# All sums of the block products on VectorE, stepped between its reads of PSUM, and one product moved behind two others

## The chip, the cores and the metric

The kernel runs on one core of one Trainium2 chip. The metric is the device time in microseconds of one execution. Before the change it is 494.15 us (median of 3 runs, 493.62 to 495.61). Profiles are of one execution; their times count from the first instruction, and the profiled span is 491.8 us.

TensorE (PE) multiplies matrices and writes to PSUM. VectorE (DVE) and ScalarE (ACT) read PSUM and work elementwise. GpSimd (POOL) works elementwise on SBUF only, and here it also issues the indirect transfers that fetch and store rows by number. SyncE (SP) issues the weight loads. Each engine runs its own instructions in the order of the program and waits for others at semaphores.

## What is computed

An attention layer of the RWKV-5 kind gives 3072 tokens of 384 features. A router then picks one of 8 experts for each token by cosine similarity, and the expert is a network of two layers:

```python
N, D, E, F = (3072, 384, 8, 1024)
...
for e in range(E):
    mask = expert_idx == e
    h = np.maximum(x[mask] @ w1[e], 0.0)
    out[mask] = gate_w[mask, None] * (h @ w2[e])
```

All values are 32-bit floats. The change concerns only these last two products, which take the kernel from about 205 us on to its end.

## The kernel before

The experts are handled one after the other as eight blocks, `blocks[0]` to `blocks[7]`, each with room for so many gathered tokens: 256 in the first two, then 448, 416, 416, 384, 384 and 384. Both layers are computed as 2x2 block products with **seven products instead of eight**, in the manner of Strassen and Winograd: sums and differences of the quarters of each operand are formed first, and the products of these are added up in PSUM and by VectorE. Only the first block's hidden layer is done plainly (`plain`), and the tokens above 256 in the second layer (`rest`).

The sums are these. S belongs to the left operand, T to the right one:

```python
def combined(eng, other, t1, t2, t3, t4, b11, b12, b21, b22):
    eng.tensor_sub(t1, b12, b11)
    other.tensor_sub(t3, b22, b12)
    eng.tensor_sub(t2, b22, t1)
    eng.tensor_sub(t4, b21, t2)

def summed_up(eng, other, s1, s2, s3, s4, a11, a12, a21, a22):
    other.tensor_add(s1, a21, a22)
    eng.tensor_sub(s2, s1, a11)
    other.tensor_sub(s3, a11, a21)
    eng.tensor_sub(s4, a12, s2)
```

Four places call them. In the profile their tiles are called Tx, Sw, Tw and Sh:

```python
def turn(self):       # transposes tokens, then Tx: sums of the tokens, for the hidden layer
    ...
        combined(nc.vector, nc.vector, *self.T, b[0][0], b[0][1], b[1][0], b[1][1])

def weigh(self):      # Sw: sums of w1, 128x512 each
    ...
    summed_up(nc.gpsimd, nc.vector, *self.S, a[0][0], a[1][0], a[0][1], a[1][1])

def weigh_out(self):  # Tw: sums of w2, 128x768 each
    ...
    combined(nc.gpsimd, nc.gpsimd, *self.T, b[0][0], b[0][1], b[1][0], b[1][1])

def halves(self):     # Sh: sums of the hidden layer's result hT, 128x512 each
    ...
    self.S = [k.cb.tile([128, NF // 2, 128], F32, name=f"Sh{j}", tag=f"Sh{j}") for j in range(4)]
    summed_up(nc.vector, nc.vector, *self.S, a[0][0], a[0][1], a[1][0], a[1][1])
```

The hidden layer goes through the weights in two rounds; `add` is a product accumulated into a bank of PSUM:

```python
def hidden(self):
    ...
    for f in range(0, NF // 2, 2):
        g = f + NF // 2
        p1, p6, p5, p7 = bank(), bank(), bank(), bank()
        add(p1, w1[:, 0, :], f, x[:, 0, one], first=True)
        p1s = kept("p1")
        nc.scalar.copy(p1s, p1)
        add(p6, self.S[1], f, self.T[1], first=True)
        u2 = kept("u2")
        vec.tensor_add(u2, p6, p1s)                      # L1049
        add(p5, self.S[0], f, self.T[0], first=True)
        p15 = kept("p15")
        vec.tensor_add(p15, p5, p1s)                     # L1052
        add(p7, self.S[2], f, self.T[2], first=True)
        p157 = kept("p157")
        vec.tensor_add(p157, p7, p15)
        add(p1, w1[:, 1, :], f, x[:, 1, one])
        add(p1, w1[:, 2, :], f, x[:, 2, one])
        nc.scalar.activation(self.hT[:, f : f + 2, one], p1, ACT.Relu)
        add(p5, self.S[3], f, x[:, 1, two])              # needs L1052's read of p5
        add(p5, w1[:, 2, :], f, x[:, 2, two])
        vec.tensor_add(self.hT[:, f : f + 2, two], p5, u2)
        relu(f, two)
        add(p7, w1[:, 1, :], g, self.T[3])
        ...
```

The second layer for the first 256 tokens:

```python
def out(self, between):
    ...
    y = [k.gp.tile([128, DM], F32, name="y", tag="y", bufs=4) for _ in range(2)]
    p1, p6, p5, p7 = bank(), bank(), bank(), bank()
    add(p1, h[:, lo, 0:128], w2[:, lo, half], first=True)
    ...
    nc.scalar.copy(p1s, p1)
    add(p6, S[1], T[1], first=True)
    vec.tensor_add(u2, p6, p1s)
    nc.scalar.mul(u21, u2, gate[1])
    nc.scalar.mul(u20, u2, gate[0])
    add(p5, S[0], T[0], first=True)
    nc.scalar.mul(p5s, p5, gate[1])
    add(p7, S[2], T[2], first=True)
    vec.scalar_tensor_tensor(u3, p7, gate[1], u21, ALU.mult, ALU.add)   # L1110
    vec.tensor_add(y[1][:, other], u3, p5s)
    add(p7, h[:, hi, 128:256], T[3])                                    # needs L1110's read of p7
    vec.scalar_tensor_tensor(y[1][:, half], p7, gate[1], u21, ALU.mult, ALU.add)
    self.put(1, y[1])
    add(p1, h[:, hi, 0:128], w2[:, hi, half])
    nc.scalar.mul(y[0][:, half], p1, gate[0])
    add(p5, S[3], w2[:, hi, other])
    vec.scalar_tensor_tensor(y[0][:, other], p5, gate[0], u20, ALU.mult, ALU.add)
    self.put(0, y[0])
    between()                        # turn of the block after next
    if self.n > 256:
        self.rest(self.n - 256)
```

The order of the whole, with `at(i)` being block i where there is one:

```python
for i in range(E):
    blocks[i].halves()
    for b in at(i + 1):
        b.hidden()
    for b in at(i + 2):
        b.weigh()
    first_weights(i + 3)
    blocks[i].out(lambda: [b.turn() for b in at(i + 2)])
    for b in at(i + 3):
        b.gather()
    for b in at(i + 1):
        b.weigh_out()
    second_weights(i + 2)
```

Of the kernel before, what the change touches and what calls it, by code (L numbers as in the profile page):

```python
# [1 line left out]

# [7 lines left out]
F32 = mybir.dt.float32  # L10
# [15 lines left out]
NF = F // 128  # L26
# [788 lines left out]
class Early:  # L815
# [44 lines left out]
    def out(self, to):  # L860
        k, nc, ps = self.k, self.k.nc, self.ps
        y = k.work.tile([128, DM], F32, name="earlyy", tag="xd")
        nc.vector.tensor_scalar_mul(y, ps, self.gate)
        nc.gpsimd.indirect_dma_start(
            out=k.out[:, :], out_offset=IndirectOffsetOnAxis(ap=to[:, self.col], axis=0), in_=y[:, :], in_offset=None,
            bounds_check=N - 1, oob_is_err=False,
        )
# [90 lines left out]
class Block:  # L958
# [14 lines left out]
    def turn(self):  # L973

        k, nc, n = self.k, self.k.nc, self.n
        self.xT = k.xtp.tile([128, NK, TM * 128], F32, name="xTe", tag="xTe")
        for m in range(NK):
            ps = k.ps.tile([128, TM * 128], F32, name="ps", tag="ps")
            for t, (G, _, _, here) in enumerate(self.tiles):
                nc.tensor.transpose(  # L980
                    ps[:, t * 128 : t * 128 + here], G[0:here, m * 128 : (m + 1) * 128], k.ident[0:here, 0:here]
                )
            nc.scalar.copy(self.xT[:, m, 0:n], ps[:, 0:n])
        if self.rank != TURN[0]:
            b = [[self.xT[:, m, s * n // 2 : (s + 1) * n // 2] for s in range(2)] for m in range(2)]
            self.T = [k.xtp.tile([128, TM * 64], F32, name=f"Tx{j}", tag=f"Tx{j}")[:, 0 : n // 2] for j in range(4)]
            combined(nc.vector, nc.vector, *self.T, b[0][0], b[0][1], b[1][0], b[1][1])

    def weigh(self):

        k, nc, w1 = self.k, self.k.nc, self.w1
        a = [[w1[:, m, s * F // 2 : (s + 1) * F // 2] for s in range(2)] for m in range(2)]
        self.S = [k.cb.tile([128, F // 2], F32, name=f"Sw{j}", tag=f"Sw{j}") for j in range(4)]
        summed_up(nc.gpsimd, nc.vector, *self.S, a[0][0], a[1][0], a[0][1], a[1][1])

    def weigh_out(self):

        k, nc, w2 = self.k, self.k.nc, self.w2
        b = [[w2[:, f * NF // 2 : (f + 1) * NF // 2, s * DM // 2 : (s + 1) * DM // 2] for s in range(2)] for f in range(2)]
        self.T = [k.cb.tile([128, NF // 2, DM // 2], F32, name=f"Tw{j}", tag=f"Tw{j}") for j in range(4)]  # L1000
        combined(nc.gpsimd, nc.gpsimd, *self.T, b[0][0], b[0][1], b[1][0], b[1][1])

    def plain(self):

# [8 lines left out]
                )  # L1013
            nc.scalar.activation(self.hT[:, f, 0:n], ps[:, 0:n], ACT.Relu)

    def hidden(self):

        k, nc, n, w1, x = self.k, self.k.nc, self.n, self.w1, self.xT
        half, vec = n // 2, self.k.nc.vector
        one, two = slice(0, half), slice(half, n)  # L1020
        self.hT = k.hp.tile([128, NF, TM * 128], F32, name="hT", tag="hT")

        def bank():
            return k.ps.tile([128, TM * 128], F32, name="ps", tag="ps")[:, 0 : 2 * half].rearrange("p (j t) -> p j t", j=2)

        def kept(name):
            t = k.ev.tile([128, TM * 128], F32, name=name, tag=name)
            return t[:, 0 : 2 * half].rearrange("p (j t) -> p j t", j=2)

        def add(ps, weights, f, moving, first=False):  # L1030
            for j in range(2):
                nc.tensor.matmul(  # L1032
                    ps[:, j, :], weights[:, (f + j) * 128 : (f + j + 1) * 128], moving,
                    start=(first and j == 0), stop=True, skip_group_check=True,
                )

        def relu(f, cols):
            h = self.hT[:, f : f + 2, cols]
            nc.scalar.activation(h, h, ACT.Relu)  # L1039
# [13 lines that stand above are left out]
            add(p7, self.S[2], f, self.T[2], first=True)  # L1053
            p157 = kept("p157")
            vec.tensor_add(p157, p7, p15)
            add(p1, w1[:, 1, :], f, x[:, 1, one])
            add(p1, w1[:, 2, :], f, x[:, 2, one])
            nc.scalar.activation(self.hT[:, f : f + 2, one], p1, ACT.Relu)
            add(p5, self.S[3], f, x[:, 1, two])
# [4 lines that stand above are left out]
            add(p7, w1[:, 2, :], g, x[:, 2, one])  # L1064
            vec.tensor_add(self.hT[:, g : g + 2, one], p7, u2)
            relu(g, one)
            add(p6, w1[:, 2, :], g, x[:, 2, two])
            vec.tensor_add(self.hT[:, g : g + 2, two], p6, p157)
            relu(g, two)

    def halves(self):

        k, nc = self.k, self.k.nc
        a = [[self.hT[:, f * NF // 2 : (f + 1) * NF // 2, t * 128 : (t + 1) * 128] for f in range(2)] for t in range(2)]
        self.S = [k.cb.tile([128, NF // 2, 128], F32, name=f"Sh{j}", tag=f"Sh{j}") for j in range(4)]
        summed_up(nc.vector, nc.vector, *self.S, a[0][0], a[0][1], a[1][0], a[1][1])

    def out(self, between):

        k, nc, S, T, h, w2 = self.k, self.k.nc, self.S, self.T, self.hT, self.w2  # L1080
        vec, half = nc.vector, slice(0, DM // 2)
# [22 lines left out]
        vec.tensor_add(u2, p6, p1s)  # L1104
        nc.scalar.mul(u21, u2, gate[1])
        nc.scalar.mul(u20, u2, gate[0])
        add(p5, S[0], T[0], first=True)
        nc.scalar.mul(p5s, p5, gate[1])
        add(p7, S[2], T[2], first=True)
        vec.scalar_tensor_tensor(u3, p7, gate[1], u21, ALU.mult, ALU.add)  # L1110
        vec.tensor_add(y[1][:, other], u3, p5s)
        add(p7, h[:, hi, 128:256], T[3])
        vec.scalar_tensor_tensor(y[1][:, half], p7, gate[1], u21, ALU.mult, ALU.add)  # L1113
        self.put(1, y[1])
        add(p1, h[:, hi, 0:128], w2[:, hi, half])
        nc.scalar.mul(y[0][:, half], p1, gate[0])
        add(p5, S[3], w2[:, hi, other])
        vec.scalar_tensor_tensor(y[0][:, other], p5, gate[0], u20, ALU.mult, ALU.add)
        self.put(0, y[0])
        between()  # L1120
        if self.n > 256:
            self.rest(self.n - 256)

    def rest(self, n):

        k, nc, h, w2 = self.k, self.k.nc, self.hT, self.w2
        mm = nc.tensor.matmul
        if n % 128:

# [9 lines left out]
        for t, (_, _, gate, here) in list(enumerate(self.tiles))[2:]:  # L1139
            ps = k.ps.tile([128, TM * 128], F32, name="ps", tag="ps")  # L1140
            if n % 128:
                at = slice((t - 2) * 128, (t - 2) * 128 + here)
                for m in range(NK):
                    nc.tensor.transpose(ps[0:here, m * 128 : (m + 1) * 128], yT[:, m, at], k.ident)
            else:
                for f in range(NF):
                    mm(ps[:, 0:DM], h[:, f, t * 128 : (t + 1) * 128], w2[:, f, :], start=(f == 0), stop=(f == NF - 1))  # L1147
            y = k.gp.tile([128, DM], F32, name="y", tag="y", bufs=4)
            nc.vector.tensor_scalar_mul(y[0:here], ps[0:here, 0:DM], gate[0:here])  # L1149
            self.put(t, y)  # L1150

    def put(self, t, y):
# [4 lines left out]
        )  # L1157


def combined(eng, other, t1, t2, t3, t4, b11, b12, b21, b22):  # L1160

    eng.tensor_sub(t1, b12, b11)  # L1162
    other.tensor_sub(t3, b22, b12)  # L1163
    eng.tensor_sub(t2, b22, t1)  # L1164
    eng.tensor_sub(t4, b21, t2)


def summed_up(eng, other, s1, s2, s3, s4, a11, a12, a21, a22):

    other.tensor_add(s1, a21, a22)  # L1170
    eng.tensor_sub(s2, s1, a11)  # L1171
    other.tensor_sub(s3, a11, a21)
    eng.tensor_sub(s4, a12, s2)


def experts(k):
# [18 lines left out]
    for b in blocks[0:2]:  # L1195
        b.gather()
        b.turn()
    blocks[1].weigh()
    blocks[0].plain()
    first_weights(2)  # L1200
    blocks[2].gather()
    blocks[0].weigh_out()
    for i in range(E):
        blocks[i].halves()
        for b in at(i + 1):
            b.hidden()
        for b in at(i + 2):
            b.weigh()
        first_weights(i + 3)
        blocks[i].out(lambda: [b.turn() for b in at(i + 2)])  # L1210
        for b in at(i + 3):
            b.gather()
        for b in at(i + 1):
            b.weigh_out()
        second_weights(i + 2)


# [184 lines left out]
```

## Time and profile before

| engine | busy, us | share of the span | instructions |
|---|---|---|---|
| TensorE | 437.6 | 89% | 3266 |
| TensorE's weight loads | 393.5 | 80% | 3266 |
| VectorE | 258.3 | 53% | 574 |
| GpSimd | 254.6 | 52% | 306 |
| ScalarE | 169.2 | 34% | 488 |

The profile page cuts the span into 40 slices of 12.3 us; a digit is the busy share of an engine in a slice in tenths, and PEclk is the clock that TensorE was granted. A line of a timeline has the start in us, the duration in us, the engine, the line of the kernel, the operation, what is written and read, how many instructions were merged, and in brackets how long the engine had been idle before and what ended that wait. A matmul of the program shows as two records, since its operands are 32-bit floats. A table of waits has the waiting engine and line, the one waited for, the sum in us, how often, and the longest. Idle time of an engine that nobody waits for costs nothing.

### The profile page before, as it was taken

What the parts mean: (1) busy time and instruction counts of PE and PEld (TensorE: products, weight loads), DVE (VectorE), ACT (ScalarE), POOL (GpSimd) and SP (SyncE); (2) the same over time, 40 slices, a digit from 0 to 9 for tenths busy, and PEclk for the clock granted to TensorE, in tenths of its full rate; (3) what the DMA queues carried; (4) which work ended last, traced back from release to release, by engine and by line L of the source; (5) the groups of instructions that cost most, each with busy time, mean ns of one, the idle gap of its engine ahead of it and who ended that gap; (6) DMA issues with size and microseconds to landing.
All of it is one profiled execution on the core that took longest, in us unless ns stands there. A gap on an engine that the chain in (4) does not pass through costs nothing. (4 is left out here: it accounts for less than half of the span.)

```text
span 491.8 us, 8850 instructions
## 1 busy us (share of the span) xinstructions
PE 437.6 (89%) x3266; PEld 393.5 (80%) x3266; DVE 258.3 (53%) x574; ACT 169.2 (34%) x488; POOL 254.6 (52%) x306
## 2 busy tenths in 40 slices
PE   8789999999999989995999999999989989399490
PEld 3678989888988887785999898998889887398370
DVE  3556766656667743446464543345464563931720
ACT  2376666555655540221234233132132122022010
POOL 7766586776668312482266463176185193701710
PEclk9999999999999999995999999999999999889797
DMA  8665555456530780231362613424442410400000
GB/s 178 129 140 124 125 130 112 105 109 130 130 81 33 283 312 12 81 110 73 129 209 74 217 47 144 129 85 145 161 113 99 145 48 33 144 1 16 31 37 19
DMA packets 93799, 54.36 MB, mean 111 GB/s; under 512 B 76937, under 2 KB 88380, under 8 KB 93746
## 3 DMA queue, kind: packets, MB, share of 16 engines
q1 hardware_dynamic: 89024, 43.85, 32.3%
q0 software_dynamic: 3296, 9.44, 5.7%
q8 instruction: 28, 0.46, 0.4%
q10 hardware_dynamic: 1426, 0.41, 0.3%
q14 instruction: 25, 0.20, 0.1%
HBM read 44.45 MB, written 9.63 MB: 110 GB/s over the span
## 5 line engine op out<-in xcount | busy, mean ns | idle before, releaser
L1154 POOL DMA_INDIRECT out_dram<-y,to x25 | 27.6, 1106 | 115.0 <-DVE y L1113 46.9
L1032 PE MATMUL ps<-xTe,w 128*128 128x192 f32 (+3 forms) x336 | 65.4, 336 | 0.0
L1032 PEld LDWEIGHTS ps<-xTe,w 128*128 128x128 f32 x336 | 58.5, 200 | 0.5
L305 ACT ACTIVATE xd<-V,diag 128x48 f32<-128x48 f32 x192 | 45.8, 321 | 19.3 <-DVE diag L297 14.9
L337 DVE TENSOR_TENSOR AT<-at,umask 128x512 f32<-128x512 f32 x48 | 30.9, 685 | 34.2 <-PE at L333 34.2
L1094 PE MATMUL ps<-Tw,Sh 128*128 128x192 f32 x192 | 34.4, 338 | 9.2 <-POOL Tw L1164 9.2
L1094 PEld LDWEIGHTS ps<-Tw,Sh 128*128 128x128 f32 x192 | 32.7, 197 | 10.4 <-POOL Tw L1164 10.4
L1039 ACT ACTIVATE hT<-hT 128x384 f32<-128x384 f32 (+3 forms) x42 | 22.0, 523 | 54.5 <-DVE hT L1061 39.9
L367 POOL TENSOR_TENSOR state<-state,wpow 48x192 f32<-48x192 f32 x40 | 20.4, 509 | 28.2 <-DVE state L363 26.7
L333 PE MATMUL at<-RT,KT 48*128 48x128 f32 x384 | 27.9, 285 | 4.4 <-ACT KT L322 3.4
L333 PEld LDWEIGHTS at<-RT,KT 48*128 48x128 f32 x384 | 23.3, 187 | 9.3 <-ACT KT L322 5.0
L898 POOL DMA_INDIRECT G<-xs,take x25 | 26.0, 1040 | 8.9 <-issue 7.0
L1032 PE MATMUL ps<-Tx,Sw 128*128 128x192 f32 (+3 forms) x168 | 29.8, 327 | 0.0
L1032 PEld LDWEIGHTS ps<-Tx,Sw 128*128 128x128 f32 x168 | 27.7, 191 | 0.2
L1032 PE MATMUL ps<-xTe,Sw 128*128 128x192 f32 (+3 forms) x56 | 13.2, 362 | 16.3 <-DVE p L1052 16.3
L383 PE MATMUL y<-AT,V 128*48 128x128 f32 x384 | 25.9, 277 | 0.0
L291 POOL TENSOR_TENSOR KU<-KU,Rpad 128x384 f32<-128x384 f32 x24 | 24.0, 1001 | 1.9
L282 POOL TENSOR_TENSOR Kpad<-K,kpow 128x384 f32<-128x384 f32 x23 | 23.0, 1001 | 3.5 <-DVE kpow L100 2.3
L1032 PEld LDWEIGHTS ps<-xTe,Sw 128*128 128x128 f32 x56 | 10.0, 209 | 18.1 <-issue 18.1
L290 POOL TENSOR_TENSOR KU<-K,u_bc 128x384 f32<-128x384 f32 x24 | 24.0, 1000 | 0.3 <-DVE diag L297 0.3
L1171 POOL TENSOR_TENSOR Sw<-Sw,w 128x512 f32<-128x512 f32 x7 | 11.4, 1631 | 24.2 <-DVE Sw L1170 16.2
L1094 PE MATMUL ps<-w,hT 128*128 128x192 f32 x128 | 23.4, 326 | 0.0
(234 smaller groups left out, 978.6 us busy)
## 6 DMA issues: line engine op xcount, KB each, us to landing
w<-in_moe_w_dram SPq DMA_DIRECT2D x16, 1536.0 KB, 6.9
K<-in_k_dram SPq DMA_DIRECT2D x24, 192.0 KB, 3.3
V<-in_v_dram SPq DMA_DIRECT2D x24, 192.0 KB, 3.6
xs<-X SPq DMA_DIRECT2D x24, 192.0 KB, 2.0
Rpad<-in_r_dram SPq DMA_DIRECT2D x23, 192.0 KB, 3.6
G<-xs,take POOLq DMA_INDIRECT x27, 3.1
out_dram<-y,to POOLq DMA_INDIRECT x25, 2.6
Rpad<-in_r_dram ACTq DMA_DIRECT2D x1, 192.0 KB, 3.8
```

Source lines behind the costliest of these rows:

```text
L282: k.nc.gpsimd.tensor_mul(k.Kpad[i % len(k.Kpad)][:, :, 0:D], k.loaded[i][0], k.kpow)
L290: nc.gpsimd.tensor_mul(KU, K, k.u_bc)
L291: nc.gpsimd.tensor_mul(KU, KU, R[:, :, 0:D])
L305: k.nc.scalar.mul(xd[:, h, :], V[:, h, :], diag[:, h : h + 1])
L333: nc.tensor.matmul(at[s][:, p, :], KT[rows, p, :], RT[rows, p, :], start=True, stop=True)
L337: nc.vector.tensor_mul(a, at[s], k.umask[:, None, :].to_broadcast([128, NP, C]))
L383: mm(y[s * DP : s * DP + D, p, :], V[:, 2 * p + s, :], AT[s][:, p, :], start=(c == 0 and p == 0), stop=True, skip_group_check=True,)
L898: nc.gpsimd.indirect_dma_start(out=G[0:n, :], out_offset=None, in_=k.xs[:, :], in_offset=IndirectOffsetOnAxis(ap=take[0:n], axis=0), bound ...
L1032: nc.tensor.matmul(ps[:, j, :], weights[:, (f + j) * 128 : (f + j + 1) * 128], moving, start=(first and j == 0), stop=True, skip_group_che ...
L1039: nc.scalar.activation(h, h, ACT.Relu)
L1094: nc.tensor.matmul(ps, a[:, f, :], b[:, f, :], start=(first and f == 0), stop=(f == NF // 2 - 1), skip_group_check=True)
L1154: k.nc.gpsimd.indirect_dma_start(out=k.out[:, :], out_offset=IndirectOffsetOnAxis(ap=k.to[0:here, j : j + 1], axis=0), in_=y[0:here, :], i ...
```

## The change

All sums go to VectorE. Those of a block's first weights (Sw) and of the hidden result (Sh) are no longer formed in one run of four: the functions become generators, and `out` takes single steps from them between VectorE's reads of PSUM. The sums of the second weights (Tw) are stepped in the same way by `hidden` of the following block. GpSimd is left with the transfers alone. Sh gets two buffers, since the next block's are now formed while the present ones are read. In `out` the product that goes on in p7's bank moves to the end, behind two others. The scaling of the remaining rows in `rest` moves from VectorE to ScalarE, and the last block's remainder is done ahead of its `out`. The aim is that no run of sums stands in front of VectorE's reads of PSUM, and that TensorE need not wait for GpSimd.

The core of the diff (cuts marked with `...`):

```diff
     def weigh(self):
...
-        summed_up(nc.gpsimd, nc.vector, *self.S, a[0][0], a[1][0], a[0][1], a[1][1])
+        yield from summed_up(nc.vector, *self.S, a[0][0], a[1][0], a[0][1], a[1][1])
     def weigh_out(self):
...
-        combined(nc.gpsimd, nc.gpsimd, *self.T, b[0][0], b[0][1], b[1][0], b[1][1])
+        yield from combined(nc.vector, *self.T, b[0][0], b[0][1], b[1][0], b[1][1])
-    def hidden(self):
+    def hidden(self, steps):
...
             vec.tensor_add(p157, p7, p15)
+            do(steps, 1)
...
             vec.tensor_add(self.hT[:, g : g + 2, two], p6, p157)
             relu(g, two)
+            do(steps, 1)
     def halves(self):
...
-        self.S = [k.cb.tile([128, NF // 2, 128], F32, name=f"Sh{j}", tag=f"Sh{j}") for j in range(4)]
-        summed_up(nc.vector, nc.vector, *self.S, a[0][0], a[0][1], a[1][0], a[1][1])
-
-    def out(self, between):
+        self.S = [k.cb.tile([128, NF // 2, 128], F32, name=f"Sh{j}", tag=f"Sh{j}", bufs=2) for j in range(4)]
+        yield from summed_up(nc.vector, *self.S, a[0][0], a[0][1], a[1][0], a[1][1])
+
+    def out(self, steps):
...
         nc.scalar.mul(u20, u2, gate[0])
+        do(steps, 2)
         add(p5, S[0], T[0], first=True)
         nc.scalar.mul(p5s, p5, gate[1])
         add(p7, S[2], T[2], first=True)
         vec.scalar_tensor_tensor(u3, p7, gate[1], u21, ALU.mult, ALU.add)
         vec.tensor_add(y[1][:, other], u3, p5s)
-        add(p7, h[:, hi, 128:256], T[3])
-        vec.scalar_tensor_tensor(y[1][:, half], p7, gate[1], u21, ALU.mult, ALU.add)
-        self.put(1, y[1])
+        do(steps, 3)
         add(p1, h[:, hi, 0:128], w2[:, hi, half])
...
         self.put(0, y[0])
-        between()
-        if self.n > 256:
-            self.rest(self.n - 256)
+        do(steps, 3)
+        add(p7, h[:, hi, 128:256], T[3])
+        vec.scalar_tensor_tensor(y[1][:, half], p7, gate[1], u21, ALU.mult, ALU.add)
+        self.put(1, y[1])
...
-            nc.vector.tensor_scalar_mul(y[0:here], ps[0:here, 0:DM], gate[0:here])
+            nc.scalar.mul(y[0:here], ps[0:here, 0:DM], gate[0:here])
...
+def do(steps, count=4):
+    for _ in range(count):
+        next(steps, None)
...
     for i in range(E):
-        blocks[i].halves()
+        doubled = blocks[i].weigh_out()
         for b in at(i + 1):
-            b.hidden()
+            b.hidden(doubled)
+        do(doubled)
+        if i == E - 1:
+            blocks[i].rest()
+        ready = [b.weigh() for b in at(i + 2)] + [b.halves() for b in at(i + 1)]
+        blocks[i].out(itertools.chain(*ready))
+        first_weights(i + 3)
         for b in at(i + 2):
-            b.weigh()
-        first_weights(i + 3)
-        blocks[i].out(lambda: [b.turn() for b in at(i + 2)])
+            b.turn()
+            do(b.Tx)
+        if 256 < blocks[i].n and i < E - 1:
+            blocks[i].rest()
         for b in at(i + 3):
             b.gather()
-        for b in at(i + 1):
-            b.weigh_out()
         second_weights(i + 2)
```

`combined` and `summed_up` lose their second engine and yield after each sum. Ahead of the loop, the second block's Sw and the first block's Sh are formed in whole on VectorE, and the first block's Tw is left to the loop.

## The prediction

> **What bounds the kernel now.** I read the share of each engine first, then the chain that ended last, then TensorE's own waits, and last the timelines of TensorE, VectorE and GpSimd around the longest of those waits. The first three rows show that TensorE is the fullest engine and that VectorE and GpSimd are only half full, so no amount of work taken off those two shortens anything by itself:
>
> ```profile
> span 491.8 us, 8850 instructions
> PE   8789999999999989995999999999989989399490
> POOL 7766586776668312482266463176185193701710
> PEclk9999999999999999995999999999999999889797
> ```
>
> The holes in the PE row (slices 19, 35 and 38) are the places to look at, and the granted clock falls in or right after each. The table of TensorE's waits over the expert stage (200 to 482 us) has engine and line waited for, sum in us, times, longest:
>
> ```profile
> PE ps L1032 <- DVE p L1052: 16.3, 6, 7.4
> PE ps L1094 <- POOL Tw L1164: 9.2, 3, 6.2
> PE ps L1094 <- DVE v L1110: 5.4, 8, 0.7
> ```
>
> So 30.9 us of the stage are waits of TensorE on VectorE and GpSimd. TensorE's timeline places the long ones and shows what follows them (start, us, then the idle time in brackets):
>
> ```profile
> 227.38 1.19 PE L1032 MATMUL ps<-xTe,Sw 128*128 128x128 f32 x4 [7.29 <-DVE p L1052]
> ...
> 418.25 0.81 PE L1032 MATMUL ps<-xTe,w 128*128 128x192 f32 x4
> ...
> 429.70 1.62 PE L1032 MATMUL ps<-xTe,Sw 128*128 128x192 f32 x4 [7.38 <-DVE p L1052]
> ...
> 465.09 5.62 PE L1094 MATMUL ps<-Tw,Sh 128*128 128x192 f32 x24 [6.19 <-POOL Tw L1164]
> ```
>
> The same four matmul records take 0.81 us at 418 and 1.62 us at 429.70: a long hole is paid twice, once as idle time and once in a slow clock after it. Why VectorE is late at 429 is in the timelines of VectorE and GpSimd:
>
> ```profile
> 418.99 0.68 DVE L1170 TENSOR_TENSOR Sh<-hT 128x512 f32<-128x512 f32 x1
> 419.71 0.69 DVE L1171 TENSOR_TENSOR Sh<-Sh,hT 128x512 f32<-128x512 f32 x1
> 420.31 6.10 DVE L1172 TENSOR_TENSOR Sh<-hT 128x512 f32<-128x512 f32 x1
> 426.34 2.28 DVE L1173 TENSOR_TENSOR Sh<-hT,Sh 128x512 f32<-128x512 f32 x1
> ...
> 420.53 1.82 POOL L1162 TENSOR_TENSOR Tw<-w 128x768 f32<-128x768 f32 x1
> 422.30 1.81 POOL L1163 TENSOR_TENSOR Tw<-w 128x768 f32<-128x768 f32 x1
> 424.06 1.80 POOL L1164 TENSOR_TENSOR Tw<-w,Tw 128x768 f32<-128x768 f32 x1
> 425.94 2.14 POOL L1165 TENSOR_TENSOR Tw<-w,Tw 128x768 f32<-128x768 f32 x1
> ```
>
> A sum of 0.68 us takes 6.10 us while GpSimd forms its sums. Behind it stand VectorE's reads of PSUM (L1049, L1052), and TensorE waits for L1052. VectorE's sums are short when GpSimd has none; its reads of PSUM keep their 0.54 to 0.62 us either way. The two engines' sums exclude each other.
>
> **What the Trainium skill says.** "SBUF — State Buffer", section "Who interferes with whom", says that a VectorE instruction with two SBUF inputs contends with a GpSimd instruction that reads SBUF, and that the loser blocks fully instead of sharing. The trace agrees (6.10 us against 0.68), but for who goes first: the record of the blocked sum begins at 420.31, before GpSimd's at 420.53. "TensorE: Matmul & The Clock Gate", section "Part 1: The HAM clock gate", says that an idle window of about 3.4 us halves the clock: the waits of 6.2 to 7.4 us are followed by doubled times, the ones of 1.6 us and less are not. "SBUF — State Buffer", section "SBUF: two separate sides", warns that VectorE can hold up GpSimd's writing of DMA descriptors. In the trace one gather among VectorE's sums took 1.50 us on GpSimd instead of 1.00; VectorE's sums beside it kept 0.68.
>
> **The change part by part.** A product of four matmuls shows as 8 records, 1.30 us at 192 columns (374.00 to 375.30). TensorE's matmuls are the same in number and shape; only their order in the second layer changes. So everything gained must come out of its holes.
>
> 1. *First block's wait (227.38).* Removed: 7.29 us idle. From 227.38 to 237.07, 64 records took 9.69 us; at the later rate (12 in 1.34 us, 0.112 each) they take 7.2, so the slow clock cost 2.5. What stays: the half-sums of the first block can only start after the last Relu (ends 217.83). Four at a spacing of 0.61 us (279.72 to 280.33) end at 220.3, and two reads of PSUM at 0.35 end at 221.0. TensorE is ready at 219.9: 1.1 us of wait stay, too short for the slow clock. Gain 7.3 + 2.5 - 1.1 = **8.7**.
> 2. *Last block's hidden layer (429.70).* Idle 7.38. The first 12 records took 3.98 us instead of 1.95, the next 12 took 2.09: 2.2 of slow clock. The half-sums now lie inside the output product of the block before. Gain **9.6**.
> 3. *Last output product (465.09).* Idle 6.2; from 465.09 to 471.38 6.29 us, against 4.73 for the same work at 443.57: 1.6. The last block's weight sums now go on VectorE, four at an estimated 0.87 us (128x192 sums are spaced 0.28, 128x512 ones 0.61, so about 1.0 ns per column), 3.5 us in all, while TensorE does two plain remainders of 5.2 us each. Gain **7.8**.
> 4. *Two smaller waits for GpSimd's Tw* (367.78 and 403.29): 1.44 + 1.60. The Tw sums are now stepped through the hidden layer before. Gain **3.0**.
> 5. *Waits on L1110*, eight of 0.67 us: the product that goes on in p7's bank started before VectorE had read p7. Two other products (2.6 us) now lie between; the read takes 0.42. Gain **5.4**.
> 6. *Small waits on L1052* (0.20, 0.29, 0.54, 0.55), made by the half-sums right ahead of u2. Gain **1.6**.
> 7. *Tail.* The last evacuation is half a row (0.42 us) instead of a whole one (0.62). Gain **0.2**.
>
> Sum: 8.7 + 9.6 + 7.8 + 3.0 + 5.4 + 1.6 + 0.2 = 36.3.
>
> What is added: 46 sums on VectorE (2 of Sw in each of 7 blocks, 4 of Tw in each of 8), and 9 row scalings of 0.6 us leave it for ScalarE. For a block of 384 tokens VectorE then has 12 reads of PSUM at 0.56 us (6.7), 8 sums at 0.61 and 4 at 0.87 (8.4), the token sums (1.4) and the output's reads (2.0): 18.5 us in a block of 35.3 (349.80 to 385.14). It does not become the bound. Nor do the steps stand in the way one by one. In a hidden step TensorE needs 2.6 us for the four first products and 1.3 for p1's rest before it needs L1052's read of p5. The step of 0.87 us from the round before ends 1.5 us in, u2 then ends at 2.0 and L1052 at 2.5, against 3.9. In the output product, with u2 read 3.2 us in, two steps end at 4.5 and p7 is complete at 5.3; then u3 and y end at 6.2, three steps at 8.1, the read of p5 at 8.5, three more steps at 10.4 and y[1] at 10.8. TensorE has gone on to transposes at 9.3, whose first Tx comes about 0.4 us late; that matters only in the two blocks without a remainder, by 0.1 at most. I allow **0.7** for all such small waits and semaphores. 36.3 - 0.7 = 35.6, and 494.15 - 35.6 = **458.5 us**.
>
> **The rivals.**
> - *VectorE's order becomes the wait.* With 12 sums of 0.6 to 0.9 us between its reads of PSUM in a block (it had 6), one bad place costs up to 0.9 us; twice a block over 7 blocks that is 12 us, so about 470. For it: these waits are in the profile even now (0.2 to 0.55 on L1052). Against it: the slacks above, 1.4 us in the hidden layer.
> - *GpSimd's transfers are held up by VectorE's sums.* Against: gathers and weight loads come about a block ahead of use (the weights land 6.8 us after issue), and the writes have no reader. Only the last write is on the end, with no sum beside it. Worth 0 to 1 us.
> - *The excess goes another way*: TensorE without holes is throttled, or the slow clock stays after the first wait. From 237 to 300 it was busy 60.91 of 63 us at a clock of 1.00, so I expect no throttle; the slow clock would cost 2.5, giving 461.
> - *The transfers bound it.* The DMA share is 0.27 to 0.45 in the stretches between 217 and 418 us; compressing them by a seventh leaves room.
>
> **Range and chances.** The parts 2, 3 and 5 (22.8 us) follow from order alone and I hold them nearly certain; part 1 and the allowance carry the doubt, some 2 us towards faster and 5 towards slower. So 455 to 463. To come out less than 2% faster (above 484.3) nearly three quarters of the gain would have to be lost: 0.02; slower 0.01.
>
> **What would show it.** TensorE's waits in the stage: L1052 down from 16.3 us to about 1, once, in the first block; the ones on Tw and on the read in the output product gone. The sums on VectorE: all Sh and Sw at 0.68, Tw near 0.95, no 6.10. Busy time: TensorE down by the 6.3 us of slow clock, GpSimd down by some 80 us (32 Tw sums x 1.9 and 14 Sw sums x 1.43). The PE row without holes after slice 20. Wrong would be: a new wait of TensorE on a step or on Tx in each block; Tw at well over 1 us; VectorE's sums stretched by GpSimd's transfers, too.

## The result and the profile after

The changed kernel takes **456.88 us** (median of 4 runs, 456.70 to 460.14) against 494.0 before (median of 4 runs, 493.62 to 495.61): a ratio of **0.9258**, 95% interval 0.9212 to 0.9305. The forecast was 458.5 us, with a range of 455 to 463. The time is right, but in part by luck: two errors in the steps that make it up, each of about 4 us, cancel.

In six of the thirteen profiles of this document, the changed kernel's among them but not that of before, TensorE's clock dips once between 175 and 185 us, ahead of everything that was changed, and 2 to 3 us go there. So I compare stages, from the first plain matmul to TensorE's last one, and from there to the end.

The head of the page after the change (share of engines; then the rows of 40 slices, now of 11.5 us):

```profile
span 458.0 us, 8806 instructions
PE 429.9 (94%) x3266; PEld 391.2 (85%) x3266; DVE 257.1 (56%) x611; ACT 174.0 (38%) x497; POOL 178.4 (39%) x260
PE   8879999999999998999999999999999999999970
POOL 7765676685675732144004114113113113200310
```

The holes of the PE row after slice 19 are gone. GpSimd lost 76.2 us (254.6 to 178.4), where some 80 were forecast. VectorE has 37 instructions more and is busy 1.2 us less (258.3 to 257.1): the time of the sums it took over is about that of the stretching and the row scalings that it lost. TensorE's waits in the same stage (columns as before):

```profile
PE ps L1033 <- DVE p L1053: 1.1, 1, 1.1
PE ps L981 <- DVE earlyy L864: 0.7, 1, 0.7
PE ps L1147 <- ACT yT L1141: 0.5, 3, 0.2
```

L1053 is the former L1052. Of the 30.9 us of waits on VectorE and GpSimd, 1.1 are left, once, in the first block; the other two lines were there before. TensorE's timeline at the places of the three long holes:

```profile
224.04 0.71 PE L1033 MATMUL ps<-xTe,Sw 128*128 128x128 f32 x4 [1.12 <-DVE p L1053]
...
400.29 0.81 PE L1033 MATMUL ps<-xTe,w 128*128 128x192 f32 x4
...
404.19 0.81 PE L1033 MATMUL ps<-xTe,Sw 128*128 128x192 f32 x4
...
435.31 4.06 PE L1097 MATMUL ps<-Tw,Sh 128*128 128x192 f32 x24
```

No bracket stands behind the last two, and the 24 records take 4.06 us where they took 5.62. VectorE's part is in the lists of the tiles (least, median and greatest duration in ns, then first and last start):

```profile
L1175 DVE TENSOR_TENSOR Sh<-hT x8: 682/684/685, 222.0 to 420.8; 128x512 f32<-128x512 f32 x8
L1167 DVE TENSOR_TENSOR Tw<-w,Tw x8: 948/948/951, 229.0 to 426.0; 128x768 f32<-128x768 f32 x8
```

L1175 is the sum that took 6.10 us. Now all eight take 0.68, and Tw takes 0.95 on VectorE against 1.8 to 2.1 on GpSimd. The short waits on L1110 are gone, too. The product that goes on in p7's bank, in the last block but one, before and after:

```profile
448.30 1.54 PE L1094 MATMUL ps<-Tw,hT 128*128 128x192 f32 x8 [0.67 <-DVE v L1110]
...
422.39 1.46 PE L1097 MATMUL ps<-Tw,hT 128*128 128x192 f32 x8
```

From the first plain matmul to TensorE's last product the stage took 273.8 us before and 233.6 after: **40.2 us less, 4 more than the parts 1 to 6 of the forecast** (36.1). From TensorE's last product to the end it took 11.1 us before and **14.7** after: 3.6 more, where the forecast had 0.2 less. GpSimd's timeline shows that end, first before the change and then after it:

```profile
477.07 0.97 POOL L1154 DMA_INDIRECT out_dram<-y,to  x1 [2.42 <-DMA out_dram<-y,to]
481.61 0.97 POOL L1154 DMA_INDIRECT out_dram<-y,to  x1 [3.57 <-DVE y L1149]
...
435.12 0.97 POOL L1157 DMA_INDIRECT out_dram<-y,to  x1 [3.06 <-ACT y L1152]
443.20 0.97 POOL L1157 DMA_INDIRECT out_dram<-y,to  x1 [7.12 <-DVE y L1120]
447.61 0.97 POOL L1157 DMA_INDIRECT out_dram<-y,to  x1 [3.44 <-DVEq L1267]
```

TensorE ends at 443.27, VectorE has the last half row ready at 443.73, but the last write starts at 447.61. It stood behind the write of 443.20: the profile names VectorE's sequencer as what ended that wait, but the kernel's third profile, below, has "3.84 <-DMA out_dram<-y,to" at the same place. Before the change the last write started 0.93 us after TensorE's end (481.61 against 480.68).

### The profile page after: what moved, and what is told of

Its sections match the earlier page's. It is cut to its first block, busy times and chain, and to the rows that moved or that the text cites. A ratio compares the mean times of both kernels' runs of the same rounds, so it can differ in the third digit from the quotient of the medians.

```text
span 458.0 us, 8806 instructions
## 1 busy us (share of the span) xinstructions
PE 429.9 (94%) x3266; PEld 391.2 (85%) x3266; DVE 257.1 (56%) x611; ACT 174.0 (38%) x497; POOL 178.4 (39%) x260
## 5 line engine op out<-in xcount | busy, mean ns | idle before, releaser
L1157 POOL DMA_INDIRECT out_dram<-y,to x25 | 30.5, 1220 | 179.7 <-issue 91.8
L1033 PE MATMUL ps<-xTe,w 128*128 128x192 f32 (+3 forms) x336 | 62.9, 327 | 0.0
L1033 PEld LDWEIGHTS ps<-xTe,w 128*128 128x128 f32 x336 | 55.9, 190 | 0.5
L338 DVE TENSOR_TENSOR AT<-at,umask 128x512 f32<-128x512 f32 x48 | 30.9, 686 | 34.2 <-PE at L334 34.2
L1097 PE MATMUL ps<-Tw,Sh 128*128 128x192 f32 x192 | 32.5, 326 | 0.0
L1097 PEld LDWEIGHTS ps<-Tw,Sh 128*128 128x128 f32 x192 | 31.4, 190 | 0.0
L1050 DVE TENSOR_TENSOR u<-ps,p 128x384 f32<-128x384 f32 (+3 forms) x14 | 7.8, 557 | 31.7 <-PE ps L1033 30.9
L490 ACT COPY xT<-xp 128x384 f32<-128x384 f32 x24 | 11.5, 479 | 31.8 <-PE xp L488 31.8
L384 PEld LDWEIGHTS y<-AT,V 128*48 128x48 f32 x384 | 19.8, 122 | 3.0
```

The costliest lines, as they stand in the source:

```text
L338: nc.vector.tensor_mul(a, at[s], k.umask[:, None, :].to_broadcast([128, NP, C]))
L384: mm(y[s * DP : s * DP + D, p, :], V[:, 2 * p + s, :], AT[s][:, p, :], start=(c == 0 and p == 0), stop=True, skip_group_check=True,)
L1033: nc.tensor.matmul(ps[:, j, :], weights[:, (f + j) * 128 : (f + j + 1) * 128], moving, start=(first and j == 0), stop=True, skip_group_che ...
L1097: nc.tensor.matmul(ps, a[:, f, :], b[:, f, :], start=(first and f == 0), stop=(f == NF // 2 - 1), skip_group_check=True)
L1157: k.nc.gpsimd.indirect_dma_start(out=k.out[:, :], out_offset=IndirectOffsetOnAxis(ap=k.to[0:here, j : j + 1], axis=0), in_=y[0:here, :], i ...
```

## The experiments

**One half of the change at a time.** The first kernel keeps the new order and steps, and puts the sums back on the engines that formed them before (two of Sw and all of Tw on GpSimd):

```diff
-    yield eng.tensor_sub(s2, s1, a11)
+    yield (slow or eng).tensor_sub(s2, s1, a11)      # slow is GpSimd for Sw
...
-        yield from combined(nc.vector, *self.T, b[0][0], b[0][1], b[1][0], b[1][1])
+        yield from combined(nc.gpsimd, *self.T, b[0][0], b[0][1], b[1][0], b[1][1])
```

> The changed kernel's order and steps, but the sums that GpSimd had before (two of Sw, all four of Tw) are on GpSimd again. Theory A (order and engine are both needed): the long stretched half-sums ahead of the hidden layer are gone, since they lie in the output product, but Tw at 1.8 us each on GpSimd stand behind its gathers and end late, so TensorE waits on Tw ahead of some output products (3 such waits before, 9.2 us) and some VectorE sums are still stretched over 1 us: 460 to 468 us. Theory B (the order is all): 457, as the changed kernel. Theory C (the two engines' exclusion is all): back near 485 to 494.

Measured: 475.29 us, ratio to before 0.9588 (0.9551 to 0.9626). TensorE's waits:

```profile
PE ps L1033 <- DVE p L1053: 7.3, 1, 7.3
PE ps L1097 <- POOL Tw L1167: 5.7, 4, 2.1
```

The waits on Tw came as expected. What the expectation of 460 to 468 forgot is the first block: its half-sums stand ahead of the hidden layer in the new order, too, GpSimd forms that block's Tw at the same time, and one sum is stretched to 5.31 us again. The first hidden layer takes 19.63 us as before (19.82), not 11.21. So both theories of a single cause fall: order alone gives about half. Its stage is 24.9 us shorter than before, and its end is 4.5 us longer. The forecast held that the parts 2, 3 and 5 follow from order alone. The last hidden layer takes 14.30 us, as in the changed kernel, and no wait on the read of p7 is listed, but the last output product still waits 1.4 us for Tw, instead of 6.2.

The second kernel does the opposite: all sums on VectorE, in their old places.

```diff
-    summed_up(nc.gpsimd, nc.vector, *self.S, a[0][0], a[1][0], a[0][1], a[1][1])
+    summed_up(nc.vector, nc.vector, *self.S, a[0][0], a[1][0], a[0][1], a[1][1])
-    combined(nc.gpsimd, nc.gpsimd, *self.T, b[0][0], b[0][1], b[1][0], b[1][1])
+    combined(nc.vector, nc.vector, *self.T, b[0][0], b[0][1], b[1][0], b[1][1])
```

> The kernel before with all sums on VectorE, in their old places in runs of four, and nothing else changed. Theory A (the engine alone gives little, the order gives the rest): no sum is stretched over 1 us, but four Tw (3.5 us) and four Sh (2.4 us) stand in one run of 5.9 us ahead of each hidden layer from the third block on; L1052 ends near 7.6 us into the layer and TensorE needs it at 3.9 to 4.5: six waits of 3 to 4 us (about 22), one of some 3.4 ahead of the last output product, one of 1.1 in the first, and the eight of 0.67 stay. Removed are about 33 us, added 28 plus some slow clock: 484 to 494. Theory B (the exclusion of the two engines is all): 462 to 466, with no wait of TensorE over 1.2 us.

Measured: 506.3 us, ratio to before 1.0209 (1.0157 to 1.026): slower than before, beyond even theory A's 494. Its waits:

```profile
PE ps L1032 <- DVE p L1052: 24.2, 7, 4.1
PE ps L1094 <- DVE v L1110: 4.6, 8, 0.6
PE ps L1094 <- DVE Sh L1171: 4.4, 1, 4.4
```

The sums are all at 0.68 and 0.95 us, so the stretching is gone, and yet TensorE idles 33 us. The waits are those expected; what was sized too small is the slow clock. TensorE's timeline at one of them:

```profile
319.41 0.87 PE L1032 MATMUL ps<-xTe,w 128*128 128x208 f32 x4
...
327.61 1.75 PE L1032 MATMUL ps<-xTe,Sw 128*128 128x208 f32 x4 [3.81 <-DVE p L1052]
...
444.90 0.92 PE L1032 MATMUL ps<-xTe,Sw 128*128 128x192 f32 x4 [3.87 <-DVE p L1052]
445.65 0.81 PE L1032 MATMUL ps<-xTe,w 128*128 128x192 f32 x4
```

A wait of 3.8 us can already be followed by doubled times. Six of the seven waits on L1052 last 3.57 to 4.05 us (the first lasts 1.12), and after five of them the granted clock is 0.50 to 0.62 for some 5 us. After the sixth, the 3.87 us at 444.90, it stays at 1.00. The hidden layers together took 137.7 us against 101.9 in the changed kernel: 35.8 more, with 24.2 of idle time listed (23.1 more). **The engine without the order is a loss; the gain of 37 us needs both.**

**The moved product alone**, in the kernel before:

```diff
-        add(p7, h[:, hi, 128:256], T[3])
-        vec.scalar_tensor_tensor(y[1][:, half], p7, gate[1], u21, ALU.mult, ALU.add)
-        self.put(1, y[1])
         add(p1, h[:, hi, 0:128], w2[:, hi, half])
...
         self.put(0, y[0])
+        add(p7, h[:, hi, 128:256], T[3])
+        vec.scalar_tensor_tensor(y[1][:, half], p7, gate[1], u21, ALU.mult, ALU.add)
+        self.put(1, y[1])
```

> The kernel before with one thing changed: the product that goes on in p7's bank is moved to the end of the output product. Theory A (a short wait costs its idle time): 8 x 0.67 = 5.4 us less, 488.6. Theory B (a short wait costs more than the profile's idle time, because the pipeline has to fill again): the output product took 10.02 us with the wait in the first block before the change and 9.10 after it, so 0.92 each, 7.4 us less, 486.6. In both the eight waits of 0.67 are gone from the table. The last two writes of the second-layer product come closer together, but the remainder follows them, so nothing is lost at the end.

Measured: 492.34 us, ratio 0.9941 (0.9915 to 0.9967): 1.6 to 4.2 us less, and both totals missed. In the output products that nothing else disturbs theory B holds: 9.10 us instead of 10.01. But part of it is given back. TensorE comes to Tw earlier and waits longer for it (10.6 us instead of 9.2), and from TensorE's last product to the end it takes 13.5 us instead of 11.1. My sentence that nothing is lost at the end was wrong by 2.4 us, where the forecast's end is off by 3.8.

**Do the places of the steps matter?** The four Tw sums of a block in one run, or in two pairs:

```diff
             vec.tensor_add(p157, p7, p15)
-            do(steps, 1)                    # pairs: do(steps, 2)
...
             relu(g, two)
-            do(steps, 1)
+            do(steps, 4)                    # pairs: do(steps, 2)
```

> The changed kernel, but the four Tw sums of a block stand in one run at the end of the hidden layer's first round, instead of one at each of four places. Theory A (the places matter, and the slack can be worked out): four sums take 3.5 us, so in a block of 384 tokens they end 4.1 us into the second round, u2 and L1053 follow at 5.2, and TensorE needs L1053's read at 3.9: a wait of 1.3 in each of three blocks, 1.1 in the two of 416, 0.9 in that of 448, 2.0 in the first; with 0.2 for filling the pipeline again some 10 us more, 467. Theory B (VectorE is half empty, so the places are of no account): no change. The second round's waits on L1053 in TensorE's table tell them apart.

> The changed kernel, but the four Tw sums stand in two pairs, both in the first round of the hidden layer. Theory A (the slack is about 1.4 us in a block of 384): the second pair ends 2.4 us into the second round, L1053 at 3.45, needed at 3.9: no wait but in the first block, where it is 0.3; so at most 0.5 us more. If each added sum ahead of a read cost its own time (theory B), 0.9 us in each of seven blocks, 6 us more.

Measured on the same chip as the unaltered kernel's second run (459.0 us): 470.32 us for the run of four, and 460.13 for the pairs. Their stages are 12.4 and 0.9 us longer. The run of four has this line among TensorE's waits:

```profile
PE ps L1033 <- DVE p L1053: 10.0, 8, 2.1
```

Its six later hidden layers grew by 1.1 (448 tokens), 1.3 and 1.3 (416) and 1.5 three times (384); worked out were 0.9, 1.1 and 1.3, and 0.2 for refilling. The first grew by 3.8, where 2.0 and 0.2 were worked out: its second wait, of 2.1 us, was followed by a clock of 0.61. The pairs' 0.9 us lie in the first hidden layer as well, where 0.3 us of wait were worked out and 0.6 measured. So theory A holds but for the first block. The slack of 1.4 us is real, and an engine that is 56% busy can still cost 12 us by the place of four instructions.

**The end.** First the last block's remainder behind its output product again, as before the change:

```diff
-        if i == E - 1:
-            blocks[i].rest()
...
-        if 256 < blocks[i].n and i < E - 1:
+        if 256 < blocks[i].n:
```

> The changed kernel, but the last block's remainder is done after its output product again. Theory A (the writes of rows stand in a line): in the changed kernel the last two writes follow each other by 4.4 us (443.20 and 447.61), because each write waits until the one before has landed, and VectorE had the second half ready at 443.73. With the remainder last, 5.2 us of TensorE lie between, as before the change (477.07 and 481.61): the last write starts about 0.9 us after TensorE's last product instead of 4.3, so 3.4 us less, 453.5 us. Theory B (what is longer at the end is the closing of the program, the same in any order): no change, 456.9. Theory C (the remainder ahead of the last product was needed to hide the last Tw sums): VectorE forms them in 3.5 us during the remainder of the block before, 5.2 us, so no wait is expected; if it were, 1 to 2 us would come back.

Measured: 457.33 us, ratio 0.9227 (0.9196 to 0.9257), which overlaps the changed kernel's interval. GpSimd's timeline:

```profile
437.93 0.97 POOL L1157 DMA_INDIRECT out_dram<-y,to  x1 [5.99 <-DVE y L1120]
442.72 0.97 POOL L1157 DMA_INDIRECT out_dram<-y,to  x1 [3.82 <-DVEq L1265]
446.03 0.97 POOL L1157 DMA_INDIRECT out_dram<-y,to  x1 [2.34 <-DMA out_dram<-y,to]
```

Theory A's line of writes is there, but it is longer than I took it for: the first two are 4.8 us apart, so the third, ready near 443.9, has to wait as well. The end shrinks from 14.7 to 13.2 only. The 3.3 us between the second and third are what a write takes to land; the 4.8 needed another cause. In the changed kernel, the view of the DMA queues from 445.2 to 446.2 us, while the write of 443.20 is under way, has these rows (queue, packets, MB, share of 16 engines):

```profile
q0 software_dynamic: 23, 0.02, 9.2%
q8 instruction: 1, 0.02, 5.8%
q14 instruction: 1, 0.01, 2.6%
```

Instructions are being fetched just then. The write of 427.12 had its 64 packets within 1 us, from 429 to 430, and no fetch beside them. The end of the program holds a branch, for tokens above an expert's room. Without that branch, which these inputs don't take (the kernel then lacks that fallback for other inputs):

```diff
-    again(n)
```

> The changed kernel unaltered, as the measure for the two others on this chip: 457 to 460 us; 4.3 us between the starts of the last two writes.

> The changed kernel without the branch at its end, which would do all tokens again if an expert had more of them than its room; with these inputs it is not taken, so the output is the same, but the kernel would be wrong for others. Theory A (the last writes land late because the fetching of instructions for that branch, which VectorE and ScalarE reach as soon as they are done, takes turns with the write's packets): the last two writes start 3.3 to 3.4 us apart, as elsewhere, instead of 4.3, and the part from TensorE's last product to the end is at least 1 us shorter. Theory B (the last two writes are 4.3 us apart for another reason): the spacing stays, and the end is shorter only by what the branch itself takes.

Measured: 451.74 us, against 457.43 for the changed kernel on that chip. The last two writes:

```profile
440.20 0.97 POOL L1157 DMA_INDIRECT out_dram<-y,to  x1 [7.12 <-DVE y L1120]
443.55 0.97 POOL L1157 DMA_INDIRECT out_dram<-y,to  x1 [2.38 <-DMA out_dram<-y,to]
```

They are 3.35 us apart, against 4.81 in the changed kernel's profile on the same chip (4.41, 4.33 and 4.81 in its three profiles; 4.3 had been expected), and no fetch is listed until they are done. Theory A holds for the spacing: 1.0 to 1.5 us of the end go with the branch. That they are the fetching among the write's packets is read from the queues: in the changed kernel a fetch of q8 lies among the packets each time, and so it does in the 4.79 us of the kernel with the remainder last, while the two writes before the change that are 3.41 us apart (473.66 and 477.07) have none of q8. Nothing was run that has the branch but not the fetches.

From TensorE's last product the end takes 9.5 us instead of 14.8; the other 3.8 lie behind the last write's start (10.1 us to the end with the branch, 6.3 without). The write's 3.35 us stay.

**A better version?** The first try mends three things: the remainder last, the moved product behind one other instead of two, and the first block's half-sums stepped in pairs inside the next hidden layer:

```diff
-    do(blocks[0].halves())
...
+        if i == 0:
+            doubled, count = itertools.chain(blocks[0].halves(), doubled), 2
```

> The changed kernel unaltered, as the measure for the three others on the same chip: a stage of 233.5 us from the first plain matmul to TensorE's last, 14 to 15 us from there to the end, 457 to 460 us in all.

> The changed kernel with three ends mended: the last block's remainder is last again; the product that goes on in p7's bank stands behind one other instead of two, so that the first write of a block's output is ready 1.3 us earlier and the writes stand further apart; and the first block's half-sums are stepped inside the next hidden layer (two a step) instead of ahead of it. Expected if the waits found are the ones that are left: the first hidden layer goes from 11.2 to about 9.9 us, no wait on the read of p7 (it ends 0.6 us ahead of need), and the part from TensorE's last product to the end goes from 14.7 to between 11.2 and 12.7: together 3.3 to 4.8 us less than the changed kernel on the same chip, 452 to 454. If the end's length has another cause than the line of writes, only 1.3 us less.

Measured: 457.93 us beside 459.0, intervals 0.9213 to 0.9271 and 0.9233 to 0.9292: not told apart. The first hidden layer went to 9.83 us as expected, but the first output product waited 0.4 us on Tw, since the pairs came too late (9.72 us instead of 9.10), and the end took 14.0: three writes in a line, 5.6 and 4.0 us apart.

The second try keeps the remainder last and the moved product behind two others, but for the last block, where it stands straight behind p7's first, so that its write starts earlier; and it gives the half-sums three, two, two and one at their places:

```diff
+            doubled, counts = itertools.chain(blocks[0].halves(), doubled), (3, 2, 2, 1)
...
         vec.tensor_add(y[1][:, other], u3, p5s)
+        if last:
+            product()
```

> The changed kernel with the remainder of the last block last again; in the last block alone the product that goes on in p7's bank straight behind p7's first, as before the change, so that the first of its three writes is ready 2 us earlier; and the first block's half-sums stepped inside the next hidden layer, three, two, two and one at its four places. Expected: the first hidden layer 9.9 us instead of 11.2, no wait on Tw in the first output product (9.1), the last output product 10.0 instead of 9.1, and the last write about 1 us after TensorE's last product instead of 4.3: in sum 1.3 - 0.9 + 3.4 = 3.8 us less than the changed kernel on the same chip. If the writes in a line still end late, 1 to 2 us less.

Measured: **455.7 us**, ratio to before 0.9196 (0.9167 to 0.9224), beside the changed kernel's 0.925 (0.9219 to 0.9281) on the same chip. The parts came as expected: first hidden layer 10.06 us, first output product 9.10, last one 9.94, and the end 11.0 instead of 14.8. The profiled spans, both without the dip, are 450.8 and 455.0 us: 4.2 less. The runs scatter by 3 us and the intervals overlap at their edges, so the 0.6% between the ratios is likely and not shown, and the 4 us rest on one profile of each: the end is 3.8 us shorter and the stage 0.3.

## Why the prediction was right, step by step

| step of the forecast | forecast, us | measured, us | from the timeline |
|---|---|---|---|
| 1 first hidden layer | 8.7 | 8.6 | 19.82 to 11.21 |
| 2 last hidden layer | 9.6 | 9.7 | 24.02 to 14.30 |
| 3 last output product | 7.8 | 7.9 | 17.92 to 9.10 (its last record ends at 9.26), without step 5's share |
| 4 two smaller waits on Tw | 3.0 | 3.8 | three output products (one with no wait listed), without step 5's share |
| 5 waits on L1110 | 5.4 | 7.4 | 10.02 to 9.10, eight times |
| 6 small waits on L1052 | 1.6 | 2.9 | five hidden layers (one with no wait listed) |
| 7 tail | 0.2 | -3.6 | 11.1 to 14.7 |

- **The long holes (1 to 3)** were sized right, with the slow clock counted from the durations after the wait. The wait that should stay in the first block, 1.1 us, is 1.12.
- **The short waits (4 to 6) were mis-sized**: I took the profile's idle time as the cost. A record of a matmul lasts 0.326 us and the next begins after 0.162, so the idle time starts counting 0.16 us late, and the first records after a wait are longer (8 in 1.54 us instead of 1.46). 0.67 + 0.16 + 0.08 = 0.91 is the 0.92 measured, and 0.54 + 0.24 the 0.78 by which two hidden layers shrank. The product moved alone shows the same 0.91 in each undisturbed output product.
- **The tail (7) failed.** I sized the last read of PSUM and not what the moved product does to the writes. Its write came right behind another, and the one waits until the other has landed: the last write started 4.34 us after TensorE's end instead of 0.93. The rival of the held-up transfers spoke of the last write with "no sum beside it" and 0 to 1 us; what held it was another write, for 3.35 us, and with the branch 1.0 to 1.5 us more.
- **The allowance of 0.7 us** for new waits of TensorE on VectorE was not needed: none is listed. The rival "VectorE's order becomes the wait" was worked out rightly but for the first block, as the run of four and the pairs show.
- **GpSimd's transfers** take longer beside VectorE's sums: the first write of an output product takes GpSimd 1.9 us in the six blocks that have such sums beside it (1.03 to 1.05 before the change), and 0.97 in the last two, which have none; but nobody waits for it. The warning that the prediction took from the Trainium skill ("SBUF — State Buffer", section "SBUF: two separate sides") is given there for VectorE's two-port modes; the sums here are plain ones of two fp32 operands, so the measurement goes beyond it.
- **No throttle came**: from 236 to 430 us TensorE is busy 193.5 of 194 us, at a clock of 1.00. Nor did the transfers bound it: their engines' mean share is 0.35 there.
- **Not tried alone** is the scaling of the remaining rows on ScalarE. The remainders took TensorE the same time before and after (8.97, 7.56, 7.56 and 5.16 us), so no gain is left for it to explain.

That the excess of 4 us in the stage and the loss of 3.8 at the end cancel is luck; the mechanism of the stage, its waits and its slow clock, was right.

## What to carry to other kernels

An engine that is half empty can still set the time by the order of its instructions: work out, at each place where the busiest engine needs a result, when the other engine gets there, and step the extra work into the slack. Moving work to a faster engine without doing so made this kernel slower. Price a short wait of TensorE, with products like the ones here, at the profile's idle time and about 0.25 us more, a long one with its slow clock, and look at what the reordering does to the last writes.

## What had not been expected of the hardware

- Instructions are fetched through the transfer engines, and at the program's end among the packets of the last writes: the next write could start 3.35 us after such a write without the branch, and 4.2 to 5.6 us after it where a fetch of q8 came in the same microsecond as its packets (nine profiles).
- The sum that is blocked has the earlier start in the records (420.31 against GpSimd's 420.53) and ends only at 426.41, 0.55 us after the end of GpSimd's third sum (425.86), so it was kept out over three of GpSimd's sums, not one. Why it is let in there was not tried.
- The slow clock can come earlier than I had read from the kernel before, where it followed waits of 6.2 us and more: in the kernel with the engine alone five of six waits of 3.57 to 4.05 us in the hidden layers brought it on (1.75 us for four records instead of 0.87) and one of 3.87 us did not, and in the run of four two waits of 1.1 and 2.1 us within 8 us were followed by it as well (up to 1.06 us for four records instead of 0.61). The Trainium skill, "TensorE: Matmul & The Clock Gate", section "Part 1: The HAM clock gate", names an idle window of about 3.4 us that runs freely, so that a wait a little longer need not hold a whole one: the six waits agree with that, the pair of short waits does not by itself.
